# Down of the last two token chunks as seven block products, in a block of attention and GEGLU

## The chip, the cores and the metric

The kernel runs on one core of a Trainium2 chip. The metric is the device time of one execution in microseconds: the median of several runs. The core's engines each run their own line of instructions in order: PE (matrix products, with a separate line PEld that loads the stationary operand), DVE and POOL (elementwise work), ACT (elementwise work with tables such as gelu and exp, copies, casts) and SP, which here only issues DMAs. They meet through semaphores.

## The reference

One transformer block in fp32 on x of 2048 tokens by 512: attention with pre-layernorm over a dilated window of eight keys, then a gated feed-forward with pre-layernorm. Cut to what is computed:

```python
def _A_ref(x, wqkv, wo):                 # 32 heads of 16
    qkv = (x @ wqkv) ...                 # q, k, v
    idx = pos[:, None] - (arange(8) * 2)[None, :]      # masked below 0
    logits = einsum("bhsd,bhswd->bhsw", q, k[idx]) * 16 ** -0.5
    o = einsum("bhsw,bhswd->bhsd", softmax(logits), v[idx])
    return o.reshape(B, S, D) @ wo

def _B_ref(x, w_gate, w_up, w_down):     # 512 -> 1792 -> 512
    return (_gelu(x @ w_gate) * (x @ w_up)) @ w_down

h  = x + _A_ref(_layernorm(x), wqkv, wo)
h2 = h + _B_ref(_layernorm(h), w_gate, w_up, w_down)   # returned
```

## The kernel before

The tokens are cut into four chunks of 512, each of four row blocks of 128; the 1792 inner features into 14 f tiles of 128 (`NF`). Chunk by chunk the kernel normalizes x, projects q, k, v, runs the attention on DVE and POOL, multiplies by wo, adds x, normalizes again (`tail`), and runs the feed-forward; the feed-forward of one chunk runs on PE beside the attention of the next.

Every fp32 operand of a matmul is split into a high part in the reduced format fp32r, by a cast on ACT (the names with h), and a low part, the rest, by a subtraction on DVE or POOL (the names with l). Each product is three matmuls: high by high, high by low, low by high. All large matmuls have a stationary operand of 128x128 and a moving one of 128x512. The splits of the weights are made once, in chunk 0, and their low parts kept in DRAM (`ld`), from where a later chunk loads them.

**Gate and up.** For chunks 0 and 1, `ffn_step` does an f tile in 24 matmuls into two PSUM banks (pg, pu), takes gelu of pg on ACT, multiplies by pu on DVE, and has g, whose parts gh and gl feed Down. For chunks 2 and 3 together `joint` goes by pairs of f tiles (seven pairs): the two tiles of a pair, the halves of the 512 inner columns and the two chunks form a two by two block product, done with seven block products for eight. Its weight sums (`sraw`, from the raw weights `fraw`) and their parts (`jh`, `jl`) are made per pair; the sums of the two chunks' normalized rows (`tt`, parts `tth`, `ttl`) are made once in `combine`, as chunk 3's `tail` ends. A block product is `product`, six matmuls at L1080; its bank is copied out or added on DVE and ACT (`jt`). For the first `EARLY` = 3 pairs, chunk 2's share of two of the products is made before (`early_step`, L1172), while chunk 3's attention runs, and kept (`m1`).

**Down.** `flush` takes an f tile whose g is ready: for each of the four row blocks three matmuls (L894 to L896) with g stationary and the 512 columns of w_down moving, added up over all 14 f tiles in four PSUM banks (`acc`), which were seeded with h by copies (`start`). `finish` copies the banks out and stores them. Chunk 2's Down runs inside `joint`; the g of chunk 3 are kept in SBUF, and chunk 3's Down is done last, alone (`rest`): per f tile w_down is loaded again, cast, and g split.

**The order.** Nothing is issued as the program is written: each instruction (or a few) is an operation with its reads and writes, and `Plan.schedule` puts them into a line per engine, always taking the ready operation of the highest rank. Before, the rank is the longest path to the end by the planner's own costs, with floors and slacks set along the program and a table `SHIFTS` that nudges stretches of operations. `SWAPS` lists operations that go to their other engine (DVE for POOL, ACT for DVE). All DMAs are on SP's line.

Of the kernel before, what the change touches and what calls it, by code (L numbers as in the profile page):

```python
# [37 lines left out]
STEP = 8160  # L38
FROM, TO = 52, 22
# [3 lines left out]
URGE = 0  # L43
FIRM = 600000
LASTROW = ("ACT", "ACT")
PAIRS = 7
EARLY = 3
FINE = (1,)
FIRST = [("x", 0), (1, 0), (1, 1), ("x", 1), (1, 2), (1, 3), ("x", 2), ("x", 3)] + [(0, k) for k in range(KD)]
SLACK = (0, 2000, 2000, 2000)  # L50
TREE = ("PDPDPDPD", "PPPPPPPP", "PPPPPPPP", "PPPPPPPP")
ONACT = ()
EXR = 605
# [8 lines left out]
LASTB = ("qp", "mm0", "mm1", "qp")  # L62
# [5 lines left out]
SHIFTS = (  # L68
    (1219, 51, "DVE POOL", 607), (1660, 47, "PE", 3380), (1220, 116, "POOL", 519), (1688, 19, "PE", 3124), (1331, 6, "PE DVE ACT POOL SP", 224),
    (1794, 14, "DVE POOL", 1456), (396, 49, "DVE", -1515), (781, 72, "PE DVE ACT POOL SP", 65), (1635, 45, "POOL", 5078), (1305, 5, "DVE POOL", 1248),  # L70
    (450, 21, "PE DVE ACT POOL SP", 64), (423, 33, "POOL", -349), (1650, 94, "PE DVE ACT POOL SP", 486), (586, 3, "DVE", -1930),
    (1690, 11, "DVE POOL", -1835), (1550, 208, "DVE", -1090), (456, 8, "DVE", 679), (1282, 3, "DVE", -9919), (2031, 13, "PE DVE ACT POOL SP", 13360),
    (432, 2, "SP", 1705), (1261, 100, "POOL", -927), (428, 26, "PE", 4811), (785, 1, "PE DVE ACT POOL SP", 5603), (1334, 300, "POOL", 1953),
    (1161, 30, "DVE", 499), (1200, 84, "SP", -1188), (866, 137, "POOL", 2449), (1715, 3, "ACT", 14894), (808, 16, "DVE", -177),
    (174, 121, "SP", -17796), (593, 37, "POOL", 446), (772, 2, "PE DVE ACT POOL SP", 4277), (1280, 285, "DVE", -348), (1334, 129, "ACT", -838),
    (2030, 35, "DVE POOL", 9076), (967, 177, "DVE", -469), (1311, 25, "POOL", 1591), (1148, 93, "DVE", -161), (1237, 40, "DVE", -1436),
    (2034, 18, "PE", 9395), (2035, 1, "PE DVE ACT POOL SP", -20912), (89, 159, "PE DVE ACT POOL SP", 1215), (701, 67, "DVE POOL", -248),
    (802, 143, "SP", 424), (549, 15, "PE DVE ACT POOL SP", 1449), (604, 3, "PE DVE ACT POOL SP", 1298), (1346, 14, "PE", -1573),
# [60 lines left out]


class Op:
    __slots__ = ("engine", "busy", "done", "emit", "deps", "next", "rank", "start", "n", "table", "nbytes", "lock", "floor", "slack", "nudge", "other")


class Plan:
# [98 lines left out]
def tile_block(ctx: ExitStack, tc: tile.TileContext, x: bass.AP, xt: bass.AP, wqkv: bass.AP, wo: bass.AP,  # L244
# [939 lines left out]
    def last_two(n):  # L1184
# [10 lines left out]
        for (f, _), keep in zip(pairs, early):  # L1195
            early_step(c, f, keep)
# [111 lines left out]
```

## Time and profile before

| | before |
|---|---|
| time, median of 3 runs | 633.44 us (632.98 to 634.53) |
| span of the profiled execution | 631.7 us |
| PE busy | 622.8 us, 99%, 2770 instructions |
| DVE busy | 484.9 us, 77%, 532 instructions |
| ACT busy | 412.1 us, 65%, 702 instructions |
| POOL busy | 387.0 us, 61%, 357 instructions |
| DMA, mean over the span | 212 GB/s |
| `joint` and chunk 3's Down | from 441.6 us to 627.7 us |

The page's own time is its span: 631.7 us for the one execution that was profiled, 1.7 us under the median of the runs, which holds what lies around the span too. A matmul is listed with some 390 ns, but the next one starts while it runs: the distance from start to start is what it costs, and that is read from a stretch with many matmuls. In the timeline by slices each digit is the busy share of a fortieth of the span (15.8 us) in tenths.

### The profile page before, as it was taken

How to read it: one execution, taken by the hardware profiler on the slowest of the kernel's cores; microseconds unless marked ns; L12 is line 12 of the kernel's file. 1: busy time of each engine (PE TensorE's matmuls, PEld its weight loads, DVE VectorE, ACT ScalarE, POOL GpSimd, SP SyncE). 2: the span in 40 equal slices, each digit the busy share in tenths (PEclk: the TensorE clock that was granted, in tenths of full speed). 3: DMA queues.
4: the chain of work that ended last, by engine and by line, in shares of the span. 5: the costliest groups of instructions: out<-in, count | busy, mean ns of one | idle time of the engine just before them, and what ended most of it. 6: DMA issues, size and time to landing. Idle time of an engine off the chain costs nothing.

```text
span 631.7 us, 8236 instructions
## 1 busy us (share of the span) xinstructions
PE 622.8 (99%) x2770; PEld 512.4 (81%) x2770; DVE 484.9 (77%) x532; ACT 412.1 (65%) x702; POOL 387.0 (61%) x357
## 2 busy tenths in 40 slices
PE   8999999999999999999999999999999999999997
PEld 7888787887888888878888888887788888888885
DVE  5979999999999899989999999968754363343421
ACT  6796696557645865996876777876555555543542
POOL 4579788434799797534594973877569775720000
PEclk9999999999999999999999999999999999999999
DMA  8666699499879968999989788941233332212772
GB/s 308 242 222 241 194 260 284 138 363 315 294 271 269 295 203 264 262 348 349 334 286 335 202 232 243 276 139 37 64 117 117 116 104 81 67 51 60 224 194 88
DMA packets 74329, 134.02 MB, mean 212 GB/s; under 512 B 32288, under 2 KB 32544, under 8 KB 73904
## 3 DMA queue, kind: packets, MB, share of 16 engines
q1 hardware_dynamic: 74288, 133.51, 66.9%
q8 instruction: 21, 0.34, 0.2%
q14 instruction: 20, 0.16, 0.1%
HBM read 99.88 MB, written 26.80 MB: 201 GB/s over the span
## 4 chain that ended last, share of the span: by engine, by line
PE 94%; DVE 3%; ACT 2%; DMA 1%; issue 0%; SPq 0%; POOL 0%; ACTq 0%; DVEq 0%; POOLq 0%
PE pu L418 12%; PE pg L418 12%; PE pa L1080 11%; PE qkv L418 9%; PE acc L894 8%; PE acc L895 8%; PE acc L896 8%; PE wo L418 7%; PE pc L1080 6%; PE qka L643 4%; PE pb L1080 2%; PE qkv L411 2%; PE qkc L643 2%; PE pg L1172 1%; PE pu L1172 1%; PE warm_ps L326 1%
## 5 line engine op out<-in xcount | busy, mean ns | idle before, releaser
L805 POOL TENSOR_TENSOR pv<-pv 128x1024 f32<-128x1024 f32 (+1 forms) x45 | 89.1, 1983 | 23.9 <-DVE pv L800 22.8
L894 PE MATMUL acc<-dnh,gh 128*128 128x512 f32 x224 | 87.4, 390 | 0.0
L896 PE MATMUL acc<-dnh,gl 128*128 128x512 f32 x224 | 87.2, 389 | 0.0
L895 PE MATMUL acc<-dnl,gh 128*128 128x512 f32 x224 | 87.2, 389 | 0.0
L756 DVE TENSOR_TENSOR pk<-kw,qp 128x2048 f32<-128x2048 f32 x32 | 72.8, 2278 | 4.5 <-DMA kw<-kv 4.1
L800 DVE TENSOR_TENSOR pv<-vw,qp 128x2048 f32<-128x2048 f32 x32 | 72.6, 2282 | 0.8
L759 DVE TENSOR_REDUCE lg<-pk 128x128 f32<-128x2048 f32 x32 | 72.7, 2278 | 0.3
L418 PE MATMUL pg<-hTh,gu 128*128 128x512 f32 x224 | 60.1, 390 | 1.2 <-ACT g L945 1.2
L418 PE MATMUL pu<-hTh,gu 128*128 128x512 f32 x224 | 59.9, 389 | 0.0
L418 PEld LDWEIGHTS pg<-hTh,gu 128*128 128x128 f32 x224 | 41.9, 188 | 10.4 <-ACT g L945 1.6
L894 PEld LDWEIGHTS acc<-dnh,gh 128*128 128x128 f32 x224 | 42.0, 188 | 8.9 <-ACT acc L298 0.2
L896 PEld LDWEIGHTS acc<-dnh,gl 128*128 128x128 f32 x224 | 42.1, 188 | 8.8
L418 PEld LDWEIGHTS pu<-hTh,gu 128*128 128x128 f32 x224 | 42.0, 188 | 8.7
L895 PEld LDWEIGHTS acc<-dnl,gh 128*128 128x128 f32 x224 | 42.0, 188 | 8.6
L340 POOL TENSOR_TENSOR gl<-g,gh 128x512 fp32r<-128x512 f32 x24 | 32.4, 1352 | 13.1 <-ACT gh L339 13.0
L339 ACT CAST gh<-g 128x512 fp32r<-128x512 f32 x42 | 26.0, 619 | 15.9 <-DVE g L951 8.0
L1112 ACT COPY jt<-pa 128x512 f32<-128x512 f32 x36 | 21.1, 586 | 22.9 <-PE pa L1080 20.8
L909 ACT CAST dnh<-fraw 128x512 fp32r<-128x512 f32 x42 | 25.9, 619 | 11.7 <-PE acc L896 6.9
L1066 POOL TENSOR_TENSOR jl<-fraw,jh 128x256 fp32r<-128x256 f32 (+1 forms) x21 | 22.4, 1071 | 17.4 <-PE pa L1080 10.3
L340 POOL TENSOR_TENSOR gu<-fraw,gu 128x512 fp32r<-128x512 f32 x20 | 26.3, 1324 | 9.9 <-ACT gu L339 9.9
L1066 POOL TENSOR_TENSOR jl<-sraw,jh 128x512 fp32r<-128x512 f32 x22 | 29.3, 1333 | 4.3 <-ACT jh L1065 4.0
L1080 PE MATMUL pa<-tt,jh 128*128 128x512 f32 x112 | 30.4, 392 | 0.8 <-ACT tt L1014 0.6
(309 smaller groups left out, 1583.0 us busy)
## 6 DMA issues: line engine op xcount, KB each, us to landing
fraw<-in_wffn_dram SPq DMA_DIRECT2D x45, 768.0 KB, 5.8
kw<-kv SPq DMA_DIRECT2D x16, 704.0 KB, 5.6
vw<-kv SPq DMA_DIRECT2D x16, 704.0 KB, 5.2
dnl<-ld SPq DMA_DIRECT2D x42, 256.0 KB, 2.9
gu<-ld SPq DMA_DIRECT2D x17, 512.0 KB, 5.3
kv<-qkvt SPq DMA_DIRECT2D x32, 256.0 KB, 3.2
ld<-gu SPq DMA_DIRECT2D x14, 512.0 KB, 5.4
x<-in_x_dram SPq DMA_DIRECT2D x16, 256.0 KB, 5.1
```

Of the source, the lines that this page charges most:

```text
L340: sub = lambda eng: eng.tensor_tensor(lo(), src(), hi().bitcast(F32), op=ALU.subtract)
L418: nc.tensor.matmul(acc(), a, b, start=(p == k == 0 and not seeded), stop=(p == n - 1 and k == KD - 1), skip_group_check=seeded)
L643: nc.tensor.matmul(acc(), a(k), b()[:, k], start=first and q == k == 0, stop=q == 2 and k == 1, skip_group_check=not first)
L756: nc.vector.tensor_tensor(pr(), k4, q2.unsqueeze(2).to_broadcast([P, 2, W, QF]), op=ALU.mult)
L759: dve(2195, lambda pr=pr, jj=jj: nc.vector.tensor_reduce(lg()[:, i, jj:jj + 2], pr().rearrange("p j w (h d) -> p j w h d", d=DH), axis=AX. ...
L800: nc.vector.tensor_tensor(pr().rearrange("p j w (h d) -> p j w h d", d=DH), v5, e5, op=ALU.mult)
L805: either(home, 256 * m, lambda eng, pr=pr, m=m: eng.tensor_tensor(pr()[:, :, 0:m], pr()[:, :, 0:m], pr()[:, :, m:2 * m], op=ALU.add), [], ...
L894: nc.tensor.matmul(a, gh()[:, sl], dh(), start=(i == 0 and not SEED), stop=False, skip_group_check=SEED)
L895: nc.tensor.matmul(a, gh()[:, sl], dl(), start=False, stop=False, skip_group_check=SEED)
L896: nc.tensor.matmul(a, gl()[:, sl], dh(), start=False, stop=(i == NF - 1), skip_group_check=SEED)
L1066: either("POOL", (hi - lo) * 256, lambda eng, src=src, v=v, W_=W_, L_=L_: eng.tensor_tensor(v(L_), src(), v(W_).bitcast(F32), op=ALU.subtr ...
L1080: nc.tensor.matmul(acc(), a[:, k], b(k), start=first and p == k == 0, stop=p == 2 and k == 1, skip_group_check=not first)
```

## The change

Down of chunks 2 and 3 is done jointly, too. The 14 f tiles are taken as the two halves of the inner size (even and odd tiles), the 512 output columns as two halves, and the two chunks as the two columns of a block product; seven block products for eight. It is transposed: a weight block of 128x128 is stationary and g, 128x512 (512 tokens), moves, so that a bank holds 128 output columns by the 512 tokens of a chunk.

- The two block products that take chunk 2's g alone (even and odd tiles) are made in `joint` as the g come, by `flush_down`, into the four old banks (`sides`): six matmuls an f tile for twelve. The seven pairs are now (0,1), (2,3), and so on.
- The other five are made after `joint`, in `last_sums`, in five passes ("ways"): 7 pairs, 2 halves of 128 columns, 3 matmuls each, 210 in all. They take sums and differences of g (`less`, DVE), each split anew (ACT, DVE or POOL), and sums of weight blocks.
- The weight sums are made in `joint` per pair (`down_sums`: four sums of 128x256, four splits, four stores to DRAM) and loaded again in `last_sums`.
- h is no longer seeded by copies. Chunk 2's and chunk 3's h go to DRAM (`hs`), chunk 3's after a transpose by DMA (`turn`), and come back; chunk 2's is transposed on its way back; `unfold` puts them in the layout of the result (`hx`), and the banks are added to it on DVE (`more`). The output of these chunks is written transposed, and turned on the host.
- `EARLY` is five: five pairs have chunk 2's share made ahead. The low parts of plain weight blocks in `joint` come by DMA from `ld`, where POOL subtracted them before.
- The ranks are no longer computed: a table `RANKS` holds one number for each operation, and `SWAPS` is new. Floors, slacks and `SHIFTS` are gone. So every engine's order is a new one, in the first three chunks too.

```diff
...
-EARLY = 3
+EARLY = 5
...
+RANKS = (
+    2221194, 2198587, 2272583, 2916000, 2497537, 2552399, 2552201, 2488295, 2549292, 2863281, 2488296, 2724370, 2867947, 2867946, 2835096, 2465784,
...
     def schedule(self):
-        for o in reversed(self.ops):
-            o.rank = max((x.rank + (o.busy if x.engine == o.engine == "PE" else o.done) for x in o.next), default=0) + o.slack
-            o.rank = max(o.rank, o.floor) + o.nudge
+        for o, rank in zip(self.ops, RANKS):
+            o.rank = rank
...
                     act(busy, lambda src=src, v=v, W_=W_: nc.scalar.copy(v(W_), src()), r, [(W_, lo)])
+                    if lo < 3:
+                        f, a = ((f0, 0), None, (f1, 2 * P))[lo]
+                        dma(lambda v=v, L_=L_: v(L_).bitcast(F32), lambda f=f, a=a, s=s: ld[f]()[:, s * D + a:(s + 1) * D],
+                            (D - a) * 4 * P, [(ld[f], None)], [(L_, lo)])
+                        continue
...
+    def less(out, a, b):
+
+        either("DVE", 512, lambda eng: eng.tensor_tensor(out[0](), a[0](), b[0](), op=ALU.subtract),
+               [x[1] for x in (a, b) if x is not out], [out[1]])
...
+    def down_sums(n, fr, S_):
+
+        (a11, a21), (a12, a22) = [[(lambda t=t, r=r: quarter(t()[:, 2], r)) for r in range(2)] for t in fr]
+        r = [(fr[0], None), (fr[1], None)]
+        for i, (t, a, b, op) in enumerate(((S_[0], a21, a22, ALU.add), (S_[0], None, a11, ALU.subtract),
+                                           (S_[1], a11, a21, ALU.subtract), (S_[0], a12, None, ALU.subtract))):
+            own = lambda t=t: both(t()[:, 2])
+            either("POOL", 256, lambda eng, own=own, a=a or own, b=b or own, op=op: eng.tensor_tensor(own(), a(), b(), op=op), r, [(t, 2)])
+            hi, lo, src = (lambda t=t: t()[:, 3].bitcast(F32R)), (lambda t=t: t()[:, 4].bitcast(F32R)), (lambda t=t: t()[:, 2])
+            split(hi, lo, src, [(t, 2)], (t, 3), (t, 4), size=256)
+            dma(lambda i=i: ws[i]()[:, n], lambda t=t: t()[:, 3:5], 256 << 10, [(t, 3), (t, 4)], [(ws[i], n)])
...
+    def part_product(acc, p, wh_, wl_, gh, gl, first, last, after=()):
+
+        def emit():
+            cols = slice(p * P, (p + 1) * P)
+            for q, (a, b) in enumerate(((wh_, gh), (wh_, gl), (wl_, gh))):
+                nc.tensor.matmul(acc(), a[0]()[:, cols], b[0](), start=first and q == 0, stop=last and q == 2, skip_group_check=True)
...
+        for p in range(2):
+            u = side[p]
+            evict(u, A[p], [(A[p], None)], [(u, None)])
+            dve(605, lambda u=u, p=p: nc.vector.tensor_tensor(u(), B[p](), u(), op=ALU.add), [(B[p], None)], [(u, None)])
...
+        ways = ((0, 0, 1, C), (3, 1, 1, C), (1, 1, 1, A), (2, 0, 0, A), (None, 1, 0, A))
+        for k, (s, x, col, acc) in enumerate(ways):
+            for i in range(n if k > 1 else 0):
+                if k == 2:
+                    less(grow[i, 1, 1], grow[i, 1, 1], grow[i, 0, 1])
+                elif k == 3:
+                    less(grow[i, 0, 0], grow[i, 1, 1], grow[i, 0, 0])
+                else:
+                    less(grow[i, 1, 0], grow[i, 1, 0], grow[i, 1, 1])
...
```

Three places in the engines' lines. The first is ACT as chunk 1's feed-forward begins, with chunk 1's attention not yet done (`qp` is the tile of exponentials, `g_1_13` the first gelu of chunk 1, `acc_1` the seeds of its banks). Before:

```order
L298 COPY acc_1_0_2710<-h_1_1304 128x512
L298 COPY h_0_1295<-acc_0_2_1469 128x512
L298 COPY acc_1_1_2723<-h_1_1304 128x512
L298 COPY acc_1_2_2726<-h_1_1304 128x512
L298 COPY acc_1_3_2735<-h_1_1304 128x512
L779 ACT_TABLE_LOAD
L779 ACTIVATE qp_412<-lg_500 128x256
L945 ACT_TABLE_LOAD
L945 ACTIVATE g_1_13_2749<-pg_1_13_2715 128x512
L749 COPY qp_412<-q_2_2_2337 128x256
```

and now:

```order
L863 COPY qp_457<-q_2_2_2336 128x256
L413 COPY h_0_1295<-acc_0_0_1555 128x512
L890 ACT_TABLE_LOAD
L890 ACTIVATE warm_68<-ms_593 128x1
L892 ACTIVATE qp_457<-lg_499 128x256
L413 COPY h_0_1295<-acc_0_3_1499 128x512
L413 COPY acc_1_1_2738<-h_1_1304 128x512
L1055 ACT_TABLE_LOAD
L1055 ACTIVATE g_1_13_2754<-pg_1_13_2718 128x512
```

The exponentials stand ahead of two copies now (L892 is what L779 was, L1055 what L945 was), where they stood right before the gelu.

The second is PE between the last transposes of chunk 3's normalized rows (`tp_h_3_3`) and the first block product of `joint` (`pa_0_0`). Before (`acc_2` are chunk 2's Down banks):

```order
L351 MATMUL tp_h_3_3_4247<-ident_70,xhat_h3_3_4233 128x128 x4
L894 MATMUL acc_2_1_3911<-dnh_2_4_3844,gh_2_4_4083 128x512
L895 MATMUL acc_2_1_3911<-dnl_2_4_3842,gh_2_4_4083 128x512
L896 MATMUL acc_2_1_3911<-dnh_2_4_3844,gl_2_4_4091 128x512
L894 MATMUL acc_2_2_3940<-dnh_2_4_3844,gh_2_4_4083 128x512
L895 MATMUL acc_2_2_3940<-dnl_2_4_3842,gh_2_4_4083 128x512
L896 MATMUL acc_2_2_3940<-dnh_2_4_3844,gl_2_4_4091 128x512
L894 MATMUL acc_2_3_3949<-dnh_2_4_3844,gh_2_4_4083 128x512
L895 MATMUL acc_2_3_3949<-dnl_2_4_3842,gh_2_4_4083 128x512
L896 MATMUL acc_2_3_3949<-dnh_2_4_3844,gl_2_4_4091 128x512
L1080 MATMUL pa_0_0_4279<-tt_1_4129,jh_0_4056 128x512 x4
L1080 MATMUL pa_0_0_4279<-tt_1_4129,jl_0_4068 128x512 x2
```

and now, first where the transposes stand (`pg_2_6`, `pu_2_6` and `pg_2_8` belong to early f tiles, `dn_0` is chunk 2's Down):

```order
L1419 MATMUL pg_2_6_4191<-hTh_2_3546,gu_2_6_3966 128x512 x2
L469 MATMUL tp_h_3_3_4243<-ident_70,xhat_h3_3_4238 128x128 x4
L1419 MATMUL pu_2_6_4211<-hTh_2_3546,gu_2_6_3966 128x512 x2
L1419 MATMUL pu_2_6_4211<-hTl_2_3568,gu_2_6_3966 128x512 x2
L1419 MATMUL pu_2_6_4211<-hTh_2_3546,gu_2_6_3966 128x512 x2
L1315 MATMUL dn_0_0_4173<-gh_2_2_3976,dn_2_3816 128x512
L1315 MATMUL dn_0_0_4173<-gl_2_2_3986,dn_2_3816 128x512
L1315 MATMUL dn_0_0_4173<-gh_2_2_3976,dn_2_3816 128x512
L1315 MATMUL dn_0_1_4185<-gh_2_2_3976,dn_2_3816 128x512
L1315 MATMUL dn_0_1_4185<-gl_2_2_3986,dn_2_3816 128x512
L1315 MATMUL dn_0_1_4185<-gh_2_2_3976,dn_2_3816 128x512
L1419 MATMUL pg_2_8_4279<-hTh_2_3546,gu_2_8_4142 128x512 x2
```

There follow the rest of the early f tile 8 (24 matmuls with the row above) and Down of f tiles 4, 6 and 8, of which this is the end, and then `joint` begins:

```order
L1315 MATMUL dn_0_0_4173<-gh_2_8_4360,dn_8_4200 128x512
L1315 MATMUL dn_0_0_4173<-gl_2_8_4369,dn_8_4200 128x512
L1315 MATMUL dn_0_0_4173<-gh_2_8_4360,dn_8_4200 128x512
L1315 MATMUL dn_0_1_4185<-gh_2_8_4360,dn_8_4200 128x512
L1315 MATMUL dn_0_1_4185<-gl_2_8_4369,dn_8_4200 128x512
L1315 MATMUL dn_0_1_4185<-gh_2_8_4360,dn_8_4200 128x512
L1197 MATMUL pa_0_0_4390<-tt_1_4079,jh_0_4353 128x512 x4
L1197 MATMUL pa_0_0_4390<-tt_1_4079,jl_0_3988 128x512 x2
L1197 MATMUL pc_0_0_4407<-tt_0_4069,jh_0_4353 128x512 x4
```

Before, 9 matmuls of 128x512 stand between the transposes and the first block product; now 54 do.

The third is the last stage of the change, where the second way ends and the third begins. PE (with the semaphores that an instruction waits for; `dn_0_0` is the bank of the even tiles' product, `dn_2_0` that of the first two ways, `last_` the split sums of g, `wl_` the weight sums):

```order
L1315 MATMUL dn_2_1_5485<-last0_h2_5525,wl_fraw1_5374 128x512
L1315 MATMUL dn_2_1_5485<-last0_h0_5545,wl_oT_l_5483 128x512
L1315 MATMUL dn_2_1_5485<-last0_l0_5557,wl_oT_l_5483 128x512
L1315 MATMUL dn_2_1_5485<-last0_h0_5545,wl_oT_l_5483 128x512
L1315 MATMUL dn_2_0_5541<-last_u0_5414,wl_r1_5527 128x512 [waits DMAHW5_49,DVE_49]
L1315 MATMUL dn_2_0_5541<-last_u0_5414,wl_r1_5527 128x512 x2
L1315 MATMUL dn_2_0_5541<-last_u0_5414,wl_r4_5351 128x512 x3
L1315 MATMUL dn_2_0_5541<-last_u1_5422,wl_r5_5452 128x512 [waits DMAHW3_49]
L1315 MATMUL dn_2_0_5541<-last_u1_5422,wl_r5_5452 128x512 x2
L1315 MATMUL dn_2_0_5541<-last_u1_5422,wl_q0_5420 128x512 [waits DMAHW2_49]
L1315 MATMUL dn_2_0_5541<-last_u1_5422,wl_q0_5420 128x512 x2
L1315 MATMUL dn_2_1_5485<-last_u0_5414,wl_r1_5527 128x512 [waits DVE_49]
```

and ACT, as it runs beside that (`ht` belongs to the transpose of h, `hx` is the result's tile, `side_h` the copy out of `dn_0_0`):

```order
L413 COPY hx_d_5551<-hb_3_5478 128x2x512 [waits DMAHW6_49]
L413 COPY hx_d_5551<-hb_3_5478 128x2x512 [waits DMAHW1_49]
L413 COPY hx_d_5551<-hb_3_5478 128x2x512 [waits DMAHW0_49]
L457 CAST last_kw1_5585<-gs_v0_5328 128x512 [waits DVE_49]
L481 COPY ht_3_5588<-hb_2_5391 128x1024 [waits DMAHW4_49,Activation_49]
L413 COPY hx_c_5533<-hb_2_5391 128x2x512
L481 COPY ht_2_5613<-hb_2_5391 128x1024
L457 CAST last_vw1_5620<-gs_v0_5328 128x512 [waits DVE_49]
L413 COPY side_h_5626<-dn_0_0_4173 128x512
L457 CAST last_pr2_5632<-gs_wo_l_5000 128x512 [waits Pool_49]
L457 CAST last_pr2_5632<-gs_wo_l_5000 128x512 [waits DVE_49]
L457 CAST last3_h2_5666<-gr_q2_5133 128x512 [waits PE_49,Activation_49,Pool_49]
```

PE waits for DVE at the row that writes `dn_2_0` with `wl_r1` (its start clears the bank that the first way filled), and in the third way for ACT's copy of `dn_0_0`. Before, none of these instructions existed: chunk 3's Down ran there from the kept g, one copy of the weights and one split of g for twelve matmuls.

275 lines of the change are left out of this document (144 added, 131 removed), and 180 rows, old and new, of tables (RANKS, SWAPS).

## The prediction

> **What bounds the kernel now.** The page's engine totals and slices, then the waits of PE, then stretches of time with the busy time of each engine.
>
> ```profile
> span 631.7 us, 8236 instructions
> PE 622.8 (99%) x2770; PEld 512.4 (81%) x2770; DVE 484.9 (77%) x532; ACT 412.1 (65%) x702; POOL 387.0 (61%) x357
> PE   8999999999999999999999999999999999999997
> PEclk9999999999999999999999999999999999999999
> GB/s 308 242 222 241 194 260 284 138 363 315 294 271 269 295 203 264 262 348 349 334 286 335 202 232 243 276 139 37 64 117 117 116 104 81 67 51 60 224 194 88
> ...
> PE warm_ps L326 <- POOL ident masks.py:199: 1.3, 1, 1.3
> PE pg L418 <- ACT g L945: 1.2, 1, 1.2
> PE qkv L418 <- ACT qkvt L709: 0.8, 2, 0.6
> PE pa L1080 <- ACT tt L1014: 0.6, 1, 0.6
> PE qkv L411 <- ACT xTh L339: 0.2, 1, 0.2
> PE pa L1080 <- ACT jt L1112: 0.2, 1, 0.2
> ```
>
> PE is busy from end to end at the full granted clock. Of 631.7 us it idles 8.9, and the longest wait behind its start is 1.2 us. So the time is the number of matmuls times their pace, plus those waits and the tail. Nothing else can make the kernel faster, and anything that makes PE wait makes it slower. The stage that is rebuilt (core 0; us, then busy us and count of PE, PEld, DVE, ACT, POOL, the clock, DMA share, GB/s):
>
> ```profile
> 445.00:542.00 97.00, 96.97 (x428) 80.30 (x429) 48.07 (x66) 52.86 (x97) 69.97 (x72) 1.00 0.31 100
> 445.00:632.00 187.00, 182.63 (x804) 150.75 (x804) 76.59 (x106) 91.34 (x164) 83.08 (x86) 1.00 0.34 106
> 590.00:632.00 42.00, 37.66 (x166) 30.70 (x164) 9.01 (x13) 16.09 (x30) 0.00 (x0) 0.98 0.58 177
> ```
>
> In the first row 428 matmuls fill 97.00 us without a gap: 0.2266 us each. That is the price of one, not the 390 ns of the page's groups, which overlap. Beside them DVE has 41% of the whole stage, ACT 49%, POOL 44%, and the last 42 us use POOL not at all.
>
> **The change, term by term.** Everything is counted from the order of the instructions and priced by rows of before.
>
> *Matmuls.* Down of two chunks was 2 x 14 x 4 x 3 = 336 matmuls; now it is 14 x 2 x 3 = 84 in the joint stage and 210 in the last one, 294. The shapes stay 128x128 by 128x512; the transposed form only swaps which operand is stationary. The early tiles move work ahead and add none. 42 fewer at 0.2266: **-9.5 us**. By 390 ns it would be -16.4; the distance from start to start decides, so I take 9.5.
>
> *The wait of 1.2 us.* The chain of waits around it:
>
> ```profile
> 276.77 2.20 DVE pv L800
> 279.04 1.28 ACT L779
> 280.33 0.39 ACT qp L779
> 280.74 1.28 ACT L945
> 282.03 0.61 ACT g L945
> 282.68 3.01 PE pg L418 x12
> ```
>
> ACT takes an exponential right before the gelu that PE needs, with a table load of 1.28 us on either side. In the new order the exponential stands two copies earlier on ACT and its table is fetched ahead by a small activation, so only gelu's load is left behind it. I take the wait as gone, **-1.2**; if the exponential's input is late again, it is 0.
>
> *The wait of 0.6 us.* It is the first joint product, waiting for the sums of chunk 3's last rows (transposes, sum, cast, split). Before, 9 matmuls stand between the transposes and it, 2.0 us; now 54, 12.2 us. That covers the chain: **-0.6**. The wait for L1112 (0.2) stays: the copy after an early pair's add still has one product beside it.
>
> *New waits in the last stage.* Each f tile pair now needs, for each of five passes, a weight sum from DRAM, a split of a g or of a difference of g, and between passes the banks must be emptied: PE waits for DVE's add at the start of the second pass, and for ACT's copy of a bank at the start of the third. Neither exists before. Those ACT copies stand behind transposes and unfoldings of h. The nearest rows:
>
> ```profile
> L367 ACT COPY a_o<-o 128x1024 uint16<-128x1024 uint16 x12 | 16.4, 1363 | 0.1
> L298 ACT COPY h<-acc 128x512 f32<-128x512 f32 x7 | 4.0, 586 | 6.6 <-PE acc L896 6.5
> L964 ACT COPY h<-acc 128x256 f32<-128x256 f32 x2 | 0.6, 375 | 0.1
> L339 ACT CAST gh<-gs_wo_l 128x512 fp32r<-128x512 f32 x4 | 2.5, 622 | 6.3 <-PE acc L895 6.3
> dnl<-ld SPq DMA_DIRECT2D x21, 256.0 KB, 2.7
> out_dram<-h SPq DMA_DIRECT2D x2, 128.0 KB, 2.2
> ```
>
> Adding up ACT's line in the new order from these durations, I find the two copies done about half a microsecond before PE comes to them: no wait, but no cover either. Lower bound 0; a gain is excluded, since nothing is there now that could be saved. Upper bound 4.1: three of the 1.36 us copies too late. Nearest are the two short waits at the joint stage's own start (0.6 and 0.2), where too ACT empties a bank for PE; I take **+0.8**.
>
> *The end.* Before, two ACT copies of 0.375 us and a 128 KB store of 2.2 us follow the last matmul; now two adds on DVE do, of which the joint stage's 128x512 adds take 0.69 us, so 0.35 for half. The first of them has an output ahead of it in the line. **+0.1**, between 0 and 0.4.
>
> *What is costed at nothing.* The casts (49 splits for 28, 28 sums of 256 columns with theirs, copies for the transposes) are on ACT, which has 96 us idle in the stage's 187: the added casts are 21 x 0.62 + 28 x 0.41 = 25 us, the eight copies of 128x1024 some 11. The DMAs are at 34% there, and 28 stores and 28 loads of 256 KB are 14 MB; at the 250 to 350 GB/s of the busy slices in the GB/s row they take some 50 us of the 187, in the shadow of PE. They are loaded passes ahead; without that cover each would cost up to 2.7. The new order in the first three chunks has the same matmuls with a busy PE: nothing, apart from the waits above.
>
> Span: 631.7 - 9.5 - 1.2 - 0.6 + 0.8 + 0.1 = 621.3. The median of the runs stands 1.7 above the profiled span, so **623.0 us**.
>
> **Rivals.** *DVE and POOL hold each other up.* Two groups of DVE and two of POOL, from 445 us (POOL's from 402) on:
>
> ```profile
> L340 DVE TENSOR_TENSOR gl<-g,gh 128x512 fp32r<-128x512 f32 x11 | 12.8, 1164 | 4.0 <-ACT gh L339 3.9
> L340 DVE TENSOR_TENSOR gl<-gs_wo_l,gh 128x512 fp32r<-128x512 f32 x4 | 2.8, 693 | 8.1 <-ACT gh L339 8.1
> L1066 POOL TENSOR_TENSOR jl<-sraw,jh 128x512 fp32r<-128x512 f32 x22 | 29.3, 1333 | 4.3 <-ACT jh L1065 4.0
> L1057 POOL TENSOR_TENSOR sraw<-fraw,fraw 128x256 f32<-128x256 f32 x11 | 8.6, 781 | 0.2
> L1015 DVE TENSOR_TENSOR ttl<-traw,tth 128x256 fp32r<-128x256 f32 x2 | 0.8, 422 | 0.1
> ```
>
> The same subtraction takes DVE 1164 ns while POOL works and 693 in the last 42 us, where POOL is idle. So the two take turns on instructions that read two operands from SBUF. From the first joint product to the end these were 37 x 0.42 + 41 x 0.69 on DVE and 74 x 0.78 + 32 x 1.33 on POOL, 144 us of 185. They become 59 and 72 on DVE, 53 and 40 on POOL: 169 us, in 732 matmuls' 166. If they exclude each other wholly, the surplus is 3 us at least; and where the fourth pass needs its differences and splits (12 DVE splits of 0.47 us delay) another 5.6 may be lost. In place of the +0.8: 625.2 to 630.8 us. For it: the two prices of one subtraction. Against it: the POOL durations already hold waiting, since its 781 and 1333 ns are means with it, and DVE takes over what POOL does slowly. The Trainium skill, page "SBUF — State Buffer", section "Who interferes with whom", has a DVE instruction with two SBUF inputs contend with a GpSimd (POOL) instruction that reads SBUF, the loser blocked for the whole instruction; the rows of 1164 and 693 ns agree. By that rule taken strictly, the sum is this rival's.
>
> *The weights' buffers turn too slowly: slower than before.* The pairs' raw weights have two buffers, so pair n+1 loads when pair n's last sum has read.
>
> ```profile
> 460.12 0.39 PE L894 MATMUL acc<-dnh,gh 128*128 128x512 f32 x1
> 464.55 0.74 POOL L1055 TENSOR_TENSOR sraw<-fraw 128x256 f32<-128x256 f32 x1 [4.35 <-DMA fraw<-in_wffn_dram]
> 472.31 0.74 POOL L1058 TENSOR_TENSOR sraw<-fraw,sraw 128x256 f32<-128x256 f32 x1 [0.61 <-DVE sraw L1056]
> 473.07 3.44 SPq L303 DMA_DIRECT2D fraw<-in_wffn_dram  x2
> 476.44 0.39 PE L894 MATMUL acc<-dnh,gh 128*128 128x512 f32 x1
> ```
>
> A turn is 8.5 us of reading (464.55 to 473.05) and 3.4 of loading, 11.9, under a pair's 16.3 on PE (460.12 to 476.44): 4.4 spare. An early pair is now 66 matmuls, 15.0 us, and four sums for Down read the same buffers, three of them one after the other in one tile, each waiting for the store before it (cast 0.41, split 0.78, store 2.7: 3.9). If they begin only when the joint sums end, the turn grows by 2 x 3.9 + 2 x 0.78 = 9.4 to 21.3, and the four turns between the five early pairs lose 4 x 6.3 - 4.4 = 21: **644 us**. It decides from a turn of 18.7 us, where 4 x 3.7 - 4.4 eats the 10.4 gained. Against it: the order has the Down sums among the joint sums, not behind them, and by hand the turn comes to about 15. Were PE to idle like that, the page "TensorE: Matmul & The Clock Gate" of the Trainium skill, section "What's actually happening", would bring the clock down to half after some 3.4 us of idling and make it worse; no wait here is that long, so no run here shows it.
>
> *More waits vanish.* All idle time of PE but the tail (8.9 - 4.0 = 4.9, the start's 1.3 included) goes, and no new wait comes: 631.7 - 9.5 - 4.9 + 1.7 = 619.0 us. For it: every line is ordered anew. Against it: most of those waits have a chain of their own behind them.
>
> *It does not pay.* New waits of some 10 us, spread, cancel the 42 matmuls: 631.5 to 635.3. Only both mechanisms above at half size would do it.
>
> **How the numbers follow.** The forecast, 620.5 to 625: 0.58. DVE and POOL, 625 to 631: 0.18. More waits vanish: 0.12. Within 0.3% (1.9 us, what a measurement of this kernel can tell from no change): 0.06. Slower, by the buffers: 0.06. Faster by over 0.3% is the sum of the first three, 0.88. The range is 618.9 to 630: the fewest waits below, nearly all of the shared DVE and POOL case above.
>
> **What would show it.** PE's count falls by 42 (2770 to 2728) and its pace stays at 0.227 between waits. Nothing is waited for at the first gelu of chunk 1 nor at the first joint product. In the last 50 us of the span PE shows waits of under 2 us in all; if there are more, their releasers tell: DVE or POOL splits for the first rival, DMA at the weight sums or at the raw weights for the second. The forecast is wrong if a pair of the joint stage takes over 15.5 us, or if a window of the first three chunks, with an unchanged count of matmuls, grew by more than a microsecond.

## The result and the profile after

The changed kernel takes 624.12 us (623.68 to 625.34), the one before 633.83 us over the runs beside it: a ratio of 0.9851, 95% interval 0.9837 to 0.9865, or 9.7 us faster. The prediction was 623.0 us and its range 618.9 to 630. The page of the changed kernel, its totals and two rows of its slices, and of PE's waits the one at the start and the two of the joint stage:

```profile
span 622.4 us, 8450 instructions
PE 614.1 (99%) x2728; PEld 503.9 (81%) x2728; DVE 541.4 (87%) x614; ACT 426.7 (69%) x743; POOL 422.6 (68%) x373
PE   8999999999999999999999999999999999999997
PEclk9999999999999999999999999999999999999999
...
PE warm_ps L444 <- POOL ident masks.py:199: 1.3, 1, 1.3
PE pa L1197 <- ACT jt L1227: 1.1, 2, 0.9
...
PE pa L1197 <- ACT jh L1177: 0.3, 1, 0.3
```

PE has 42 instructions less, is as full as before and never idles for more than 1.3 us. DVE went from 77% to 87%. The two waits that were to go, 1.2 us for the first gelu of chunk 1 and 0.6 us for the first joint product, are gone. New ones stand at L1197, in the joint gate and up.

Stretches of time place the difference. First the whole stage from the first joint product on, before the change, then the same of the changed kernel, and of it the 62 us that hold the end of the joint stage and the five passes nearly to their last matmul (us, then busy us and count of PE, PEld, DVE, ACT, POOL, clock, DMA share, GB/s):

```profile
441.60:631.70 190.10, 185.82 (x816) 152.84 (x816) 79.98 (x113) 92.65 (x167) 84.13 (x88) 1.00 0.35 107
```

```profile
449.20:622.40 173.20, 167.83 (x733) 136.57 (x731) 133.71 (x190) 103.83 (x194) 104.47 (x93) 1.00 0.63 197
...
556.00:618.00 62.00, 62.00 (x274) 51.18 (x274) 49.97 (x56) 36.91 (x58) 36.28 (x24) 1.00 0.81 232
```

Up to the first joint product the changed kernel needs 7.6 us more (449.2 for 441.6): two more early pairs with their Down are 42 matmuls more there, 9.5 us, less some 1.9 us of waits that vanished. From there on it has 84 matmuls less, 19.0 us, but gains only 16.9 (173.2 for 190.1): 2.1 us go to new waits. (The list of waits shows 1.4 us there for 0.2 before; the rest are stops too short for the list, and matmuls that start a little late after a stop.) Sum: 9.3 us of span. The last row says where those waits are not: in the five passes PE is busy for 62.00 of 62.00 us. They lie earlier, in the joint stage, most of them where its pairs turn. The chain of waits around the largest:

```profile
451.40 7.66 DMA fraw<-in_wffn_dram
...
459.19 1.01 POOL sums_kw L1168
460.20 0.92 POOL sums_vw L1169
461.13 1.16 POOL sums_vw L1170
...
463.46 1.67 PE pa L1197 x6
```

The second pair's raw weights are issued at 450.01 and 451.40 us, the second of the two tiles lands at 459.06, three sums on POOL follow, casts on ACT behind them, and PE waits 0.3 us for a cast of them and then 0.9 us for a copy that stands behind such a cast (by the starts of its matmuls it loses 0.4 and 1.1 us there, the figures that the expectations below use). Of the chain two things can be disputed: that the weights come late (theory C, the prediction's second rival in small), or that the sums take long because DVE and POOL hold each other up (theory D, its first rival, in another place).

### The profile page after: what moved, and what is told of

The parts are those of the page before. It is cut to its first block, busy times and chain, and to the rows that moved or that the text cites. A ratio compares the mean times of both kernels' runs of the same rounds, so it can differ in the third digit from the quotient of the medians.

```text
span 622.4 us, 8450 instructions
## 1 busy us (share of the span) xinstructions
PE 614.1 (99%) x2728; PEld 503.9 (81%) x2728; DVE 541.4 (87%) x614; ACT 426.7 (69%) x743; POOL 422.6 (68%) x373
## 4 chain that ended last, share of the span: by engine, by line
PE 88%; DMA 4%; DVE 3%; ACT 2%; issue 1%; POOL 1%; SPq 0%; DVEq 0%; ACTq 0%; POOLq 0%
PE pg L544 12%; PE pu L544 12%; PE qkv L544 10%; PE dn L1315 10%; PE pa L1197 8%; PE wo L544 7%; PE pc L1197 5%; PE acc L1006 4%; PE acc L1004 4%; PE acc L1005 4%; PE qka L766 3%; DMA fraw<-in_wffn_dram 2%; PE pg L1419 2%; PE qkv L537 2%; PE pu L1419 1%; PE qkc L766 1%
## 5 line engine op out<-in xcount | busy, mean ns | idle before, releaser
L917 POOL TENSOR_TENSOR pv<-pv 128x1024 f32<-128x1024 f32 (+1 forms) x44 | 84.8, 1931 | 19.5 <-DVE pv L912 18.6
L1004 PE MATMUL acc<-dnh,gh 128*128 128x512 f32 x112 | 43.6, 389 | 0.0
L1005 PE MATMUL acc<-dnl,gh 128*128 128x512 f32 x112 | 43.6, 389 | 0.0
L1006 PE MATMUL acc<-dnh,gl 128*128 128x512 f32 x112 | 43.6, 389 | 0.0
L1197 PE MATMUL pa<-tt,jh 128*128 128x512 f32 x112 | 30.3, 392 | 0.3 <-ACT jh L1177 0.3
L544 PE MATMUL pg<-hTl,gu 128*128 128x512 f32 x112 | 30.1, 390 | 0.0
L544 PE MATMUL pu<-hTl,gu 128*128 128x512 f32 x112 | 29.9, 389 | 0.0
L544 PE MATMUL qkv<-wh,xTh 128*128 128x512 f32 x96 | 25.8, 393 | 0.3 <-ACT qkvt L828 0.3
L917 DVE TENSOR_TENSOR pv<-pv 128x512 f32<-128x512 f32 (+1 forms) x20 | 25.6, 1284 | 0.2
L544 PE MATMUL qkv<-wl,xTh 128*128 128x512 f32 x96 | 25.7, 389 | 0.0
L544 PE MATMUL qkv<-wh,xTl 128*128 128x512 f32 x96 | 25.5, 392 | 0.0
L1197 PEld LDWEIGHTS pa<-tt,jh 128*128 128x128 f32 x112 | 20.8, 188 | 5.6 <-ACT jh L1177 0.9
```

The costliest lines, as they stand in the source:

```text
L544: nc.tensor.matmul(acc(), a, b, start=(p == k == 0 and not seeded), stop=(p == n - 1 and k == KD - 1), skip_group_check=seeded)
L917: either(home, 256 * m, lambda eng, pr=pr, m=m: eng.tensor_tensor(pr()[:, :, 0:m], pr()[:, :, 0:m], pr()[:, :, m:2 * m], op=ALU.add), [], ...
L1004: nc.tensor.matmul(a, gh()[:, sl], dh(), start=(i == 0 and not SEED), stop=False, skip_group_check=SEED)
L1005: nc.tensor.matmul(a, gh()[:, sl], dl(), start=False, stop=False, skip_group_check=SEED)
L1006: nc.tensor.matmul(a, gl()[:, sl], dh(), start=False, stop=(i == NF - 1), skip_group_check=SEED)
L1197: nc.tensor.matmul(acc(), a[:, k], b(k), start=first and p == k == 0, stop=p == 2 and k == 1, skip_group_check=not first)
```

## The experiments

Each kernel is the changed one (624.12 us) with one edit, unless said otherwise. The times are medians; single executions spread by some 2 us.

**Is it the number of matmuls?** One pass was done twice:

```diff
-                part_product(acc[p], p, *w2[i], *g2[i], k == 0 and i == 0, i == n - 1)
+                part_product(acc[p], p, *w2[i], *g2[i], k == 0 and i == 0, i == n - 1, times=2 if k == 1 else 1)
```

> The changed kernel with every product of the second of the five last passes done twice: 42 matmuls of 128x512 more, nothing else changed (the result counts that product double). Theory A, that the time is the number of matmuls times 0.2266 us plus PE's few waits: 624.1 + 9.5 = 633.6 us, back at the time before the change. Theory B, that the last stage is set by DVE and POOL, which take turns: the added matmuls fill time that is set elsewhere, 624 to 629 us.

634.04 us, ratio to the kernel before 0.9998 (0.9988 to 1.0008), span 632.0 for 622.4: 9.6 us in the profiles for 42 matmuls, 0.229 us each. The gain is given back to a tenth of a per cent. Theory A holds, and nothing else limits the last stage as it stands.

**How much room is behind PE?**

```diff
-            for q, (a, b) in enumerate(((wh_, gh), (wh_, gl), (wl_, gh))):
+            for q, (a, b) in enumerate(((wh_, gh), (wh_, gl), (wl_, gh))[:only]):       # only = 1 in the five passes
```

> The changed kernel with the five last passes cut to one matmul of three (high by high alone; the low parts are still made, but not multiplied): 140 matmuls fewer, 31.7 us of PE. It asks how much room the other engines leave behind PE. Theory A with ample cover: 624.1 - 31.7 = 592.4 us. Theory B, that DVE stands right behind PE (in the trace of the changed kernel it works without a gap from 575 to 612.6 us and idles 5.1 us before its last adds): only some 5 to 7 us come free, 617 to 619 us.

619.2 us. Of the 31.7 us taken from PE 4.9 came out. The waits of PE in this kernel, and the stretch of the passes:

```profile
PE dn L1315 <- ACT last_vw L457: 8.6, 1, 8.6
PE dn L1315 <- DVE hx_d L1341: 5.0, 2, 4.3
PE dn L1315 <- ACT last_u L457: 3.7, 2, 2.5
...
575.00:612.00 37.00, 19.68 (x55) 13.26 (x55) 36.52 (x41) 21.52 (x34) 22.14 (x15) 0.72 0.77 224
```

DVE is busy for 36.5 of 37 us. So in the five passes the splits and differences of g are a second bound that lies only some 5 us behind PE's (a little more, if the slower matmuls told of in the last section took part of what came free): theory B is wrong for this kernel as it is, and right for any that takes 5 us more from PE there.

**Do late raw weights make PE wait?** The last reading of the first pair's weights was put some 5 us later, and the loads with it:

```diff
+        picked = [plan.ops[n] for n in (2081, 2082, 2083, 2101, 2100, 2084)]    # last sum for Down, its split, loads, store
+        # ... placed behind operation 2057 in the finished order
```

> The changed kernel with one thing moved: the last of the first pair's sums for Down on DVE, with its split, its store and the loads of the next two raw weight tiles that wait for it, stands behind two other DVE operations, some 5 us later (its end goes from 449.95 to about 455). Theory C, that the waits of 0.4 and 1.1 us at 460 and 462 us come from raw weights that return late: the later of the two loads is issued some 4 us later, so PE waits about 4 to 5 us more: 628 to 629 us. Theory D, that those waits come from DVE and POOL holding each other up: no change, 624.1 us within 0.5.

628.26 us (0.9911, 0.9897 to 0.9925), 4.1 us more. The chain of waits, and then PE's waits from 455 to 470 us:

```profile
456.06 6.17 DMA fraw<-in_wffn_dram
...
462.36 0.96 POOL sums_kw L1168
```

```profile
PE pa L1197 <- ACT jt L1227: 2.0, 1, 2.0
PE pa L1197 <- ACT jh L1177: 1.0, 1, 1.0
PE pa L1197 <- DVE jl L1183: 0.2, 1, 0.2
```

The later of the two loads is issued at 456.06 for 451.40 and lands at 462.2 for 459.1 (it is faster, perhaps since less else is under way; this was not tried), and the waits there grow from 1.2 to 3.2 us, with more at the next turns. The three sums were not stretched more than before: they took 2.5 us (462.36 to 464.89) for 3.1. So this turn of the two weight buffers has no room left: what is lost in it comes out at PE. That is theory C's price, and theory D's expectation of no change fails.

**The same weights released earlier.** Three of the first pair's sums were put some 3 us earlier on POOL, one of them taken from DVE:

```diff
+        plan.swap(2059)                                                          # DVE to POOL
+        picked = [plan.ops[n] for n in (2059, 2060, 2062)]                       # sums for up, first pair
+        # ... placed behind operation 2024 in the finished order
```

> The changed kernel with one thing moved the other way: three of the first pair's sums for gate and up stand some 3 us earlier in POOL's line, where POOL idled 3.65 us, and the first of them goes from DVE to POOL. The raw weights' last reading ends at about 449.7 us for 451.4. Theory C (late raw weights): the later load is issued some 1.5 us earlier and the waits at 460 and 462 us shrink by 1 to 1.5 us: 622.6 to 623.1 us. Theory D (DVE and POOL hold each other up): POOL now works beside DVE's splits for the first joint product, so nothing is gained and up to 0.7 us lost: 624.1 to 624.8 us.

624.01 us (0.9843, 0.9825 to 0.986): no change. The edit did not do what it was made for. Three rows of DVE's line in it:

```profile
445.98 0.96 DVE L458 TENSOR_TENSOR sums_kw<-sums_kw 128x256 fp32r<-128x256 f32 x1
446.87 1.22 DVE L458 TENSOR_TENSOR gl<-gr_r,gh 128x512 fp32r<-128x512 f32 x1
448.02 1.82 DVE L1183 TENSOR_TENSOR jl<-sraw_q,jh 128x512 fp32r<-128x512 f32 x2
```

With POOL now at work beside it, these rows take longer than in the changed kernel, where they took 0.42, 0.69 and 1.29 us. So DVE reached the last reading later than was meant, and the later load went out at 451.04 us, only 0.36 earlier. It then took 8.45 us for 7.66 and landed at 459.50, 0.4 later than in the changed kernel. On theory C the run says nothing; it shows theory D's mechanism eating what was to be won, and that the same load doesn't always take the same time.

**Less work beside POOL's sums.** The second pair's sums for Down were cut to one or two columns:

```diff
+            few = (lambda x: (lambda: x()[:, :, 0:1])) if n == 1 else (lambda x: x)
+            if n == 1:
+                hi, lo, src = [(lambda v=v: v()[:, 0:2]) for v in (hi, lo, src)]
```

> The changed kernel with the second pair's four sums for Down and their splits cut to one or two columns of 256 (their stores stay; the result is wrong by that pair's weight sums). DVE then hardly works beside POOL's chain of sums at 459 to 462 us, whose three rows took 1.01, 0.96 and 1.19 us for 0.74 at the least. Theory D (DVE and POOL hold each other up): the chain is 0.9 us shorter and the waits of 0.4 and 1.1 us shrink by about 0.9: 623.2 us. Theory C (late raw weights): the raw weights land as before at 459.06 us, and the waits stay within 0.3 us: 623.8 to 624.1 us.

622.85 us (0.9834, 0.9817 to 0.985), 1.3 less than the changed kernel, and in the profile not one wait of PE is left at the turns. The three sums on POOL:

```profile
457.97 0.76 POOL L1168 TENSOR_TENSOR sums_kw<-sums_kw,fraw 128x256 f32<-128x256 f32 x1 [1.33 <-DMA fraw<-in_wffn_dram]
458.69 0.74 POOL L1169 TENSOR_TENSOR sums_vw<-fraw,fraw 128x256 f32<-128x256 f32 x1
459.39 0.73 POOL L1170 TENSOR_TENSOR sums_vw<-fraw,sums_kw 128x256 f32<-128x256 f32 x1
```

They end 2.15 us after their start, where they took 3.08: 0.93 shorter, theory D's 0.9. The weights landed 1.2 us earlier too in this execution, 0.4 of it because all of the program stood 0.4 earlier, so the whole of the 1.3 is not D's. The profiled execution was also the fastest of the five (621.68 us), and the interval overlaps with the changed kernel's: the two are told apart here by the trace rather than by the time.

**Can the sums change places?** Those three sums to DVE, ahead of its other work, and the first sum for Down with its split to POOL in exchange:

```diff
+        for n in (2103, 2104, 2105, 2140, 2142): plan.swap(n)                    # three to DVE, two to POOL
+        # (2104, 2105) behind 2103; 2141 behind 2110; (2142, 2143) behind 2148
```

> The changed kernel with the second pair's first sums divided anew: the three sums for gate and up that PE waits for at 460 and 462 us (1.01, 0.96 and 1.19 us on POOL) go to DVE, where such a sum takes 0.42 us, and stand ahead of its other work; in exchange the first sum for Down and its split go to POOL, behind. The result stays the same. Theory D (DVE and POOL hold each other up, and POOL is the slow one): the chain of three is done at about 460.5 us for 462.3, the waits of 0.4 and 1.1 us vanish: 622.5 to 623 us. Theory C (late raw weights alone): the weights land at 459 us as before, and the waits shrink by 0.3 at most: 623.8 us.

625.17 us (0.9871, 0.9857 to 0.9885), and the unaltered kernel, run beside it:

> The changed kernel once more, unaltered, beside the run before, so that differences of a microsecond are read on one chip. Theories C and D both: 624.1 us within 0.8, with waits of PE at the turns of the pairs (around 460, 477, 508 and 544 us) that differ from one execution to the next.

623.77 us (0.9842, 0.9828 to 0.9856). So the exchange made it no faster, if anything 1.4 us slower, and theory D's 622.5 to 623 us did not come. The rows of the exchange, DVE's three with the add that follows them, the first of POOL's two, and an activation on ACT that takes that add:

```profile
457.77 0.43 DVE L1168 TENSOR_TENSOR sums_kw<-sums_kw,fraw 128x256 f32<-128x256 f32 x1 [1.81 <-DMA fraw<-in_wffn_dram]
458.11 0.97 DVE L1169 TENSOR_TENSOR sums_vw<-fraw,fraw 128x256 f32<-128x256 f32 x1
459.00 0.96 DVE L1170 TENSOR_TENSOR sums_vw<-fraw,sums_kw 128x256 f32<-128x256 f32 x1
459.88 0.68 DVE L1219 TENSOR_TENSOR gs_v<-pc,jt 128x512 f32<-128x512 f32 x1
457.81 0.98 POOL L1296 TENSOR_TENSOR sums_kw<-fraw,fraw 128x256 f32<-128x256 f32 x1 [1.24 <-DMA fraw<-in_wffn_dram]
460.59 0.63 ACT L1222 ACTIVATE gs_v<-gs_v 128x512 f32<-128x512 f32 x1 [1.74 <-DVE gs_v L1219]
```

The three sums end 2.19 us after their start, 0.9 sooner than on POOL (3.08), but later than was expected: a sum of 0.42 us takes 0.97 on DVE as long as POOL works too, so the two alternate at POOL's pace. The Trainium skill, page "SBUF — State Buffer", section "Who interferes with whom", has a DVE instruction with two SBUF inputs contend with a GpSimd (POOL) instruction that reads SBUF, and the one that issues second wait until the first has finished; the rows agree. The 0.9 us did not reach PE. The wait for the first cast went, but the add that the gelu takes (`gs_v`) now stands behind the three sums on DVE, ACT idled 1.74 us for it, and the copy behind it on ACT made PE wait 0.6 us in the old wait's place. So the exchange moved the lateness into another line. That such an exchange can never win is not shown; in the run before this one, where instructions were taken away instead, no such wait is listed.

The unaltered kernel in its second profile bears on theory C. POOL's first sum behind the late weight tile:

```profile
458.06 1.02 POOL L1168 TENSOR_TENSOR sums_kw<-sums_kw,fraw 128x256 f32<-128x256 f32 x1 [1.17 <-DMA fraw<-in_wffn_dram]
```

It starts 1.1 us earlier than in the first profile (459.19 there), because the tile took 6.89 us from issue to landing and not 7.66, and because all of the program stood 0.4 earlier. The three sums were stretched less (1.02, 0.74 and 0.93 us, 2.6 in all for 3.1), and no wait of PE is listed from 455 to 470 us. It then had 1.3 us of waits at later turns, and the same span. So the lateness of the weights and the stretch of the sums add up to a wait at a turn. The run with the later release shows that lateness by itself costs PE; what the stretch costs by itself is not shown, since in every run in which it was smaller the weights landed at another time, too. Each turn has about a microsecond to spare or to lack, and which one lacks it differs from one execution to the next.

**Was it the place of the exponential?** It was put back to right before the gelu, behind the two copies:

```diff
+        picked = [plan.ops[n] for n in (1277, 1278, 1279)]                       # table load ahead, exponential, its sum
+        # ... placed before operation 1365, the gelu
```

> The changed kernel with the exponential of chunk 2's first attention step put back to right before chunk 1's first gelu on ACT, behind the two copies, as it stood before the change. My prediction's reading, that the place in ACT's line made the wait of 1.2 us: the wait comes back, 625.3 us. The other reading, that the exponential's input came late on DVE (in the trace of the changed kernel DVE has it done at 275.2 us, where it came at 279.0 before): ACT has 0.8 us idle there and the gelu still ends before PE needs its bank, 624.1 us, no wait at 281 us.

624.34 us (0.9854, 0.9835 to 0.9873), with 0.3 us of wait at that gelu for the 1.2 of before. The times can't tell the two readings apart; the trace can. ACT's first table load in this run:

```profile
277.20 1.28 ACT L890 ACT_TABLE_LOAD   x1
```

The order on ACT is that of before, but its first table load begins at 277.20 us, where it began at 279.04 before. What ACT had waited for then was not the exponential's input, though my expectation says so. The rows of before, with the input (POOL) and what the profile names as the end of the wait (DVE), and then the same two instructions in the changed kernel:

```profile
275.64 0.74 POOL L774 TENSOR_TENSOR lg<-lg,ms 128x256 f32<-128x256 f32 x1 [1.18 <-DVE ms L773]
276.68 2.28 DVE L800 TENSOR_TENSOR pv<-vw,qp 128x2048 f32<-128x2048 f32 x1
279.04 1.28 ACT L779 ACT_TABLE_LOAD   x1 [1.20 <-DVE pv L800]
```

```profile
271.43 2.28 DVE L912 TENSOR_TENSOR pv<-vw,qp 128x2048 f32<-128x2048 f32 x1
...
274.31 0.85 DVE L887 TENSOR_TENSOR lg<-lg,ms 128x256 f32<-128x256 f32 x1
```

Before, the input was there at 276.38 us, and ACT went on 0.08 us after DVE's product `pv` had ended at 278.96. In the changed kernel that product stands ahead of the input's row in DVE's line and has ended at 273.7, and the input is there at 275.16. So what removed the wait is mostly the new order on DVE; the place of the exponential on ACT is worth the 0.3 us that came back. Why the exponential has to wait for that product was not looked for.

**What is the new order worth?** The work of both kernels was ordered by the rule of before (computed ranks, floors and slacks), without the table of nudges or ranks and with every operation on its home engine:

```diff
-        for o, rank in zip(self.ops, RANKS):
-            o.rank = rank
+        for o in reversed(self.ops):
+            o.rank = max((x.rank + (o.busy if x.engine == o.engine == "PE" else o.done) for x in o.next), default=0) + o.slack
+            o.rank = max(o.rank, o.floor) + o.nudge
-SWAPS = (57, 60, ...)
+SWAPS = ()
```

> The change's work with the order rule of before: ranks computed as the longest path to the end, with the floors and slacks that the program had, but without the table of ranks and with no operation sent to its other engine. To be compared with the kernel before treated the same way. Theory A (the count of matmuls is what pays): the difference of the two is -9.5 us within 3. Theory E (the order chosen anew is what pays, and without it the new sums and splits are not hidden): this one is no faster than the other, or slower. Its own time can't be foreseen well; waits of 10 to 60 us more than the ordered kernel's.

> The kernel before without its table of nudges and with no operation sent to its other engine: ranks, floors and slacks as they stand. Theory A: 9.5 us (within 3) slower than the changed kernel's work under the same rule. Theory E: no slower than that one.

The change's work takes 707.67 us, the work of before 688.03 us: the change is 19.6 us slower, theory E. From the first joint product to the end it now needs 201 us (503 to 704), the other 191 (494.9 to 685.5), with 84 matmuls less. PE's waits in those stretches, first of the change's work, then of the work before:

```profile
PE pa L1050 <- POOL jl L1036: 9.0, 8, 3.1
PE pa L1050 <- ACT jh L1030: 7.3, 8, 2.8
PE dn L1168 <- DVE hx_d L1194: 2.4, 1, 2.4
PE pa L1050 <- ACT jt L1080: 0.4, 1, 0.4
```

```profile
PE acc L847 <- ACT acc L251: 0.4, 1, 0.4
```

The old stage fits under PE in this order as well. The new one doesn't: there DVE is busy for 105 us for 72 in the old one's stretch, and POOL for 115 for 94, with the same two weight buffers. Up to the first joint product the change's work needs 8.1 us more, but 42 matmuls more, 9.5 us, stand there: the loss is the rebuilt stage's, 10.4 us more where 84 matmuls less should have saved 19.0. With each kernel's own choice of engines given back, and only the ranks by the old rule:

> The change's work under the order rule of before (computed ranks, floors and slacks, no table), but with the changed kernel's own choice of engine for each operation (DVE or POOL, ACT or DVE). With neither it took 707.7 us. Theory E1, that the order within the lines carries the cover of the new work: still 690 us or more. Theory E2, that the choice of engine does, by dividing the instructions that DVE and POOL can't do side by side: 640 to 670 us.

> The kernel before without its table of nudges, but with its own choice of engine. With neither it took 688.0 us. Theory E1: 675 us or more. Theory E2: 640 to 660 us. Either way the difference to the changed work under the same rule says whether that work, without an order fitted to it, is faster (count of matmuls: -9.5 us) or slower (19.6 us slower without both).

691.01 and 668.54 us. Over the whole program the choice of engine is worth 16.7 and 19.5 us, the order within the lines 67 (691.0 to 624.1) and 35 (668.5 to 633.8). By its time the change's run is within E1; for the kernel before, 668.5 lies between the two expectations. The stages say where these sums lie. From the first joint product to the end: the change's work with every operation on its home engine, the same with its own choice of engines, and the work of before with its own choice:

```profile
503.00:704.00 201.00, 177.68 (x733) 138.68 (x731) 104.90 (x152) 105.50 (x196) 115.16 (x131) 0.97 0.54 171
506.50:688.10 181.60, 169.89 (x733) 136.13 (x731) 141.56 (x193) 104.19 (x194) 103.07 (x90) 1.00 0.61 191
475.20:667.90 192.70, 188.56 (x816) 154.49 (x816) 79.20 (x113) 93.29 (x167) 84.82 (x88) 0.99 0.32 104
```

With its own engines and the old rule the rebuilt stage takes 181.6 us, 11.1 less than the old one treated the same way. So of the 28 us between 201.0 and the 173.2 of the changed kernel, the choice of engines brings 19.4 and then the order 8.4 (put back one after the other): in the stage that was rebuilt, it is E2's reading that holds. What makes 691 us is the first three chunks, which end at 506.5 us here, at 475.2 in the other run and at 449.2 in the changed kernel. Their work is nearly the same but for the early matmuls, and the floors and slacks were fitted to the kernel before; which places in them cost the time was not taken apart.

## Why the prediction was right, and where it was not

The sum forecast a span of 621.3 us; it is 622.4. Term by term:

- **The matmuls, -9.5.** Right. The count fell by 42, and 42 put back cost 9.6 us in the profile. The price from a stretch without gaps (0.2266) and not the listed 390 ns was the choice that carried the number.
- **The wait of 1.2 us.** Gone, as said, but mostly for another reason than the step gave: the place on ACT accounts for 0.3 us of it, and the earlier place of a product on DVE for the rest, as far as the trace tells.
- **The wait of 0.6 us.** Gone; that the 54 matmuls cover its chain was argued from the order and not tried by itself.
- **New waits of 0.8 in the last stage.** Wrong place and too small. The two waits there that I named did not come, nor any other. In the joint stage PE's starts lost 2.1 us more than before. That the sum still came within 1.1 us is in part luck: 0.8 us had been put down for waits that did not come. The step that failed is the one that put the pairs' turn among the unlikely, as a rival that is either 21 us or nothing. It took the load at 3.4 us from a row of before (473.07 us) that merges the issues of two tiles and says nothing of their landing. From issue to landing the raw weights took, from 440 to 500 us before and from 449 to 520 us in the changed kernel:

```profile
DMA to landing us min/median/max: 4.2/4.6/6.0
DMA to landing us min/median/max: 4.3/5.8/7.7
```

The two tiles of 768 KB of the second pair, behind stores and other loads, took 9.1 us from the first issue to the last landing. The turn of the buffers was 16.9, 14.8, 16.0 and 16.9 us by the loads' issues (450.01, 466.92, 481.73, 497.70, 514.61). On PE 66 matmuls, from the first joint product on, took 17.1, 15.0, 15.0 and 15.5 us (starts at 449.22, 466.33, 481.29, 496.25 and 511.79) for 15.0 without a stop. I had named 15.5 us a pair as the point where the forecast breaks: the first of these stretches is well over it, the last just at it, and so it came to about 2 us in all.
- **The end, +0.1.** From the last matmul's end to the end of the span 4.04 us, 4.01 before.
- **What was costed at nothing.** In the five passes the cover held, with 5 us to spare, which the prediction did not price. The new order and the new choice of engines were costed at nothing too, apart from two waits, and that was its weakest line: with the old rule and the home engines the same work is 19.6 us slower than the old. The sum was right because the lines were fitted to this work, in the rebuilt stage by the choice of engines above all, and the rows of before alone could not have shown that they would be; the gapless PE of the kernel before was no evidence for the new stage.
- **The first rival**, DVE and POOL in the last stage, was rightly not the forecast, but for the wrong reason: they do hold each other up, DVE has hardly a gap there (36.5 of 37.6 us from 575 us on), and the lines keep them just under PE.

## What to carry to other kernels

Where one engine has no gaps, price its removed instructions by the distance from start to start, and then ask of each other engine how far it lies behind: take work away from the bound and see how much of it comes out, here 4.9 of 31.7 us. A trade of matmuls for sums and splits is paid from the room of the other engines, so it has to be judged together with the division of that work among the engines and its order: the same arithmetic was 9.7 us faster with both fitted to it and 19.6 us slower with neither. For a pair of buffers, add up issue, landing under the traffic of that moment, reading, and the stretch by a neighbour engine, since a load's time in a quiet stretch is not its time in a busy one; and take the landing from a view that gives it, not from the row of the issue.

## What was unexpected of the hardware

In the kernel with 140 matmuls fewer, PE idles for 4.3 us between two passes, where it never idles for more than 1.3 us in the changed kernel. Rows of PE's timeline behind it (start, duration, count and the idle time before), and then the 6 us from 580 us on, with the granted clock third from the end:

```profile
579.70 1.65 PE L1315 MATMUL dn<-last_u,wl_r 128*128 128x512 f32 x3 [4.26 <-DVE hx_d L1341]
...
584.57 0.63 PE L1315 MATMUL dn<-last_u,wl_o 128*128 128x512 f32 x1
585.00 0.63 PE L1315 MATMUL dn<-last_kw,wl_lg 128*128 128x512 f32 x1
580.00:586.00 6.00, 5.22 (x12) 3.33 (x12) 6.00 (x7) 4.64 (x7) 4.30 (x4) 0.51 1.12 335
```

For some 6 us after the idling matmuls start 0.43 us apart, then 0.23 again, and the granted clock is 0.51. (From 575 to 612 us, which holds a stop of 8.6 us and shorter ones more, its mean is 0.72.) The Trainium skill, page "TensorE: Matmul & The Clock Gate", section "What's actually happening", has the clock fall to half after an idle window of about 3.4 us and come back after as long a busy one; the run agrees in the halving, and its slow stretch was longer, some 6 us with small gaps in it. In the change's work under the old rule shorter waits did it, too: after one of 1.1 and one of 2.1 us, 2.2 us apart, the clock was 0.50 from 571.8 to 575.2 us, while after one of 2.6 us it was 1.00 from 529.3 to 532.7 us. A bound that starts to make PE wait can thus be paid twice once its waits are long: in that run the rebuilt stage is 31 us longer than its matmuls (201.0 less 733 matmuls at 0.2266 and 4.1 at the end), and the waits listed above are 19.1 of these.
